# The q, k and v loads of twelve head pairs issued from ScalarE's queue instead of SyncE's, with new ranks for the order of all instructions

## The chip, the cores and the metric

The kernel runs on one core of a Trainium2 chip. The metric is device time in microseconds (us) from the start to the end of one execution. A core has five engines that work side by side, each through its own list of instructions in order: TensorE (PE in the profile, with its weight loads shown apart as PEld), VectorE (DVE), ScalarE (ACT), GpSimd (POOL) and SyncE (SP). SyncE computes nothing; its list consists of transfers (DMA) that it issues, and the profile shows it as SPq. A transfer issued by ScalarE stands in ScalarE's own list, among its computations (ACTq). All transfers run on the core's 16 DMA engines.

## What is computed

Attention over 4 batches of 8 heads, with q averaged over pairs of rows, and a gated two-layer network on its output:

```python
B, H, S, D = 4, 8, 1152, 64
q_pool = q.reshape(B, H, S // 2, 2, D).mean(axis=3)
scores = np.matmul(q_pool, k.transpose(0, 1, 3, 2)) / np.sqrt(D)
attn = softmax(scores)                    # over the last axis, 1e-9 added to the sum
x = np.matmul(attn, v).transpose(0, 2, 1, 3).reshape(2304, 512)
h = x @ w_in                              # w_in: 512 x 2048
out = (h * sigmoid(1.702 * h)) @ w_out    # w_out: 2048 x 512
```

Inputs and output are float32.

## The kernel before

The 32 heads are taken as 16 pairs (P = 0 to 15, four to a batch), and each pair is cut into nine score tiles of up to 128 rows by 1152 keys: n = 9P to 9P + 8, 144 in all. Pairs 0 to 3 ("wide") work in float32 and transpose on TensorE. Pairs 4 to 15, the **twelve later pairs**, split each operand into two float16 parts and transpose by DMA.

For a later pair the work is this. `q_load`, `k_load` and `v_load` bring q (three DMAs), k and v (one each) from memory into `qraw` (one buffer), `kraw` (one buffer) and `vraw` (two buffers). `q_add` (GpSimd, L448) adds the row pairs of q. Maxima and scales follow on VectorE, then the splits `q_hi`, `k_hi`, `v_hi` and `q_lo`, `k_lo`, `v_lo`. `q_tr` and `k_tr` are DMA transposes issued by SyncE (L547, L543), into `qT` and `kT`. A new `q_load` may start only when the former pair's `q_tr` has read `qraw`, and a `k_load` when the former `k_lo` has read `kraw`.

For each score tile n there follow: S (scores, TensorE, L693 for the later pairs), M (scaling, copy out of PSUM and row maximum, VectorE, L707), B (a small addition, ScalarE, L740), E (exponential, ScalarE, L714), H (`p_hi`, the high float16 part into a buffer `hl`, four buffers, ScalarE, L257), L (`p_lo`, the low part into the same buffer, GpSimd or VectorE, L748), T (`p_tr`, a DMA transpose of `hl` into `pt`, issued by SyncE, L761). When four tiles are transposed, `pv` (TensorE, L774) multiplies them with v.

Between these, TensorE works on the network: `h` pieces (six matmuls, L996) and `o` pieces (three matmuls, L1032), 288 of each. They need whole batches of x, so they fill gaps of a later pair's attention, and what is left of them runs behind the last score tile. ScalarE and VectorE do the gate (`tanh` L1004, `gate` L1010, `g_hi`, `g_lo` L1021), and SyncE stores the output (L1047).

The order on every engine is fixed before the program runs. The class `Plan` holds all pieces of work with an estimated duration, what they come after, the buffers they take and a rank; `Plan.order` simulates the engines and, whenever one is free, gives it the piece of the lowest rank among those that can start soon. The table `rank` says how far a kind of work stands ahead of or behind its tile; `movable` lists the kinds that may go to another engine; `wait` and `slack` are further weights of that simulation. In the program each engine then executes its list strictly in order and waits at each piece for what it needs. So a load in SyncE's list starts only when all transposes ahead of it have been issued, and each of those waits for its L.

Of the kernel before, what the change touches and what calls it, by code (L numbers as in the profile page):

```python
# [141 lines left out]
def kernel(  # L142
# [26 lines left out]
    nc = tc.nc  # L169
# [17 lines left out]
    rank = dict(  # L187
        w1=1865.4109269161, w1_rate=669.6352215416, w2=2677.1753665833, w2_rate=0.0023087894,
        w1_cut=1631.5317541564, w1_cut_rate=613.7055382454, w2_cut=-32.5791686736, w2_cut_rate=30.5602451484,
        v_max=860.0945280997, load=-14.5343009418, prep=556.0904376951, max=-2582.9885400672,  # L190
        exp=972.7441165849, p_hi=284.2709380703, p_lo=2243.1182350523, pv=1142.4802547388, x=925.9243816604,
        recip=2446.2725570035, w_tr=228.0055134896, w_ev=1267.7732570402, g=-1700.558705141,
        pv_b=-1144.7706645013, max_b=1484.9170056827, p_lo_b=1438.9279995691, prep_b=-2262.503153536,
        v=1284.3640449616, lift=75.4772111863,
    )
    movable = dict(DVE=('w_ev', 'v_hi', 'moe_hi', 'q_hi'), POOL=('p_lo', 'denom'))
    wait = dict(PE=0.071466, ACT=0.063566, DVE=0.051711, POOL=1.725535)
    slack = dict(PE=0.100951, ACT=1.016305, DVE=1.084473, POOL=1.138194, SP=1.01349, stay=1.645697, land=1.035543)
    sizes = dict(
# [142 lines left out]
    for i in range(32):  # L342
        c, kk = divmod(i, 4)
        j = c // 4
        first, last = i % 16 == 0, i % 16 == 15
# [59 lines left out]
    def heads(x, g):  # L405
        return x[g.b, 2 * g.pr:2 * g.pr + 2]

    def k_head(queue, g, a):
        queue.dma_start(out=T["kraw", g.P][:, a], in_=heads(k, g)[a].rearrange("(p r) d -> p r d", r=KR))

    def k_load(g):
        t = new("kraw", ("kraw", g.P), [128, 2, KR, D], F32)
        if g.P:
            nc.sync.dma_start(
                out=t.rearrange("p a r d -> p a (r d)"), in_=heads(k, g).rearrange("a (p r) d -> p a (r d)", r=KR)
            )
            return
        k_head(nc.scalar, g, 0)

    def q_load(g):  # L420
        t = new("qraw", ("qraw", g.P), [128, NJ, 2, D], F32)
        full, last = heads(q, g)[:, 0:1024], heads(q, g)[:, 1024:S]
        if g.P:
            nc.sync.dma_start(
                out=t[:, 0:8].rearrange("p (a j) r d -> p a (j r d)", a=2),
                in_=full.rearrange("a (p x) d -> p a (x d)", x=8),
            )
        else:
            for a, queue in enumerate((nc.sync, nc.scalar)):
                queue.dma_start(  # L430
                    out=t[:, 4 * a:4 * a + 4].rearrange("p j r d -> p (j r d)"),
                    in_=full[a].rearrange("(p x) d -> p (x d)", x=8),
                )
        for a in range(2):
            nc.sync.dma_start(
                out=t[64 * a:64 * (a + 1), NJ - 1].rearrange("p r d -> p (r d)"),
                in_=last[a].rearrange("(i r) d -> i (r d)", r=2),
            )
# [127 lines left out]
    def v_load(g):  # L566
        t = new("vraw", ("vraw", g.P), [128, 2, KR, D], F32)
        nc.sync.dma_start(
            out=t.rearrange("p a r d -> p a (r d)"), in_=heads(v, g).rearrange("a (p r) d -> p a (r d)", r=KR)
        )  # L570
# [26 lines left out]
    for g in pairs:  # L597
        n0, G = g.n0, g.P
# [6 lines left out]
        for i, what in enumerate("qkv"):  # L605
            key = (what + "raw", G)
            at, after = n0 + rank["load"] + 0.1 * i, [("E", n0 - 14 + i)] if n0 > 14 else []
            if what == "v" and g.wide:
                at, after = n0 + rank["v"] - 4, [("E", n0 - 5)] if n0 >= 5 else [("k_load", 0)]
            fn = dict(q=q_load, k=k_load, v=v_load)[what]  # L610
            plan.add(
                (what + "_load", G), "ACT" if what == "k" and not G else "SP", (2.9 if what == "q" else 1.6) if G > 3 else 1.6 if what == "q" else 0.8, at,
                lambda g=g, fn=fn: fn(g), after, take=[(what + "raw", key)], dma=2.0,
# [563 lines left out]
```

## Time and profile before

| | us |
|---|---|
| median of three runs (796.25 to 797.83) | 797.82 |
| the profiled execution: its own time | 796.32 |
| its span in the trace | 794.5 |
| TensorE busy | 757.8 (95%) |
| VectorE busy | 581.8 (73%) |
| ScalarE busy | 593.7 (75%) |
| GpSimd busy | 269.8 (34%) |

The profiled execution took 1.8 us more than its span, for what lies around the traced instructions, and 1.5 us less than the median of the runs. "Busy" of TensorE covers the whole of each matmul in the pipeline, so it is no measure of how near the engine is to its peak. Transfers are not busy time of the engine that issues them: the span of a DMA instruction on SPq or ACTq is the time that the queue was occupied with issuing it, and "landing" is when its data has arrived. The clock of TensorE was at its higher level, 2.4 GHz, almost throughout (0.995 in the mean).

In time the execution has three parts: pairs 0 to 3 with the preparation of the weights up to about 165 us, the later pairs from there to the last scores at 658 us, and the rest of the network to the end.

### The profile page before, as it was taken

What the parts mean: (1) busy time and instruction counts of PE and PEld (TensorE: products, weight loads), DVE (VectorE), ACT (ScalarE), POOL (GpSimd) and SP (SyncE); (2) the same over time, 40 slices, a digit from 0 to 9 for tenths busy, and PEclk for the clock granted to TensorE, in tenths of its full rate; (3) what the DMA queues carried; (4) which work ended last, traced back from release to release, by engine and by line L of the source; (5) the groups of instructions that cost most, each with busy time, mean ns of one, the idle gap of its engine ahead of it and who ended that gap; (6) DMA issues with size and microseconds to landing.
All of it is one profiled execution on the core that took longest, in us unless ns stands there. A gap on an engine that the chain in (4) does not pass through costs nothing.

```text
span 794.5 us, 16688 instructions
## 1 busy us (share of the span) xinstructions
PE 757.8 (95%) x6716; PEld 510.4 (64%) x6716; DVE 581.8 (73%) x915; ACT 593.7 (75%) x1005; POOL 269.8 (34%) x172
## 2 busy tenths in 40 slices
PE   6999999899999999889999998899999999999998
PEld 4556555457676767566666675567676766766664
DVE  5977898988978978668878787898889675222222
ACT  5987998989897979787888878776889786232222
POOL 2231323145566553455433233323535243000000
PEclk9999999999999999999999999999999999999999
DMA  8543343738999999999999999999999979010000
GB/s 307 194 135 114 137 140 133 193 88 178 224 185 198 208 208 204 215 203 215 184 214 198 206 197 196 222 190 227 199 221 192 176 120 176 1 28 2 28 1 26
DMA packets 331309, 128.75 MB, mean 162 GB/s; under 512 B 310496, under 2 KB 312544, under 8 KB 331232
## 3 DMA queue, kind: packets, MB, share of 16 engines
q1 hardware_dynamic: 330944, 127.13, 78.7%
q8 instruction: 52, 0.85, 0.4%
q10 hardware_dynamic: 288, 0.56, 0.2%
q14 instruction: 25, 0.20, 0.1%
HBM read 45.09 MB, written 4.72 MB: 63 GB/s over the span
## 4 chain that ended last, share of the span: by engine, by line
PE 63%; DMA 11%; ACT 9%; DVE 7%; issue 5%; SPq 2%; POOL 2%; DVEq 0%; ACTq 0%; POOLq 0%
PE h L996 16%; PE o L1032 15%; PE s L693 7%; DMA pt<-hl 7%; PE pv L774 6%; PE pv L809 5%; PE s L664 4%; PE o L786 4%; DVE p L707 2%; ACT p L714 2%; ACT hl L257 2%; PE h L313 2%; POOL hl L748 2%; PE tr L821 1%; DMA qraw<-in_q_dram 1%
## 5 line engine op out<-in xcount | busy, mean ns | idle before, releaser
L748 POOL TENSOR_TENSOR hl<-p,hl 128x1152 f16<-128x1152 f32 x72 | 177.4, 2467 | 180.1 <-ACT hl L257 160.2
L707 DVE TENSOR_SCALAR_CACHE_REDUCE p<-s,e_s 128x1152 f32<-128x1152 f32 x144 | 203.2, 1411 | 29.6 <-PE s L693 16.0
L1032 PE MATMUL o<-wbuf,g 128*128 128x512 f16 x864 | 205.0, 379 | 0.0
L996 PEld LDWEIGHTS <-wbuf 128*128 128x128 f16 x1728 | 168.9, 98 | 40.3 <-issue 4.9
L714 ACT ACTIVATE p<-p,nm 128x1152 f32<-128x1152 f32 x144 | 180.1, 1251 | 4.9 <-DVE p L707 1.2
L257 ACT ACTIVATE hl<-p 128x1152 f16<-128x1152 f32 x108 | 124.6, 1155 | 24.4 <-DMA pt<-hl 23.7
L1032 PEld LDWEIGHTS <-g 128*128 128x128 f16 x864 | 83.3, 98 | 84.9 <-issue 1.4
L693 PE MATMUL s<-kT,qT 128*128 128x384 f16 (+1 forms) x720 | 123.5, 327 | 10.2 <-DVE p L707 10.1
L996 PE MATMUL h<-x16a,wbuf 128*128 128x256 f16 x960 | 115.7, 273 | 1.6 <-DVE gf L1010 1.2
L1010 DVE SCALAR_TENSOR_TENSOR gf<-th,h 128x512 f32<-128x512 f32 x72 | 49.2, 684 | 91.2 <-ACT th L1004 91.1
L1004 ACT ACTIVATE th<-h,t_s 128x512 f32<-128x512 f32 x72 | 49.0, 681 | 83.0 <-PE h L996 82.7
L693 PEld LDWEIGHTS <-qT 128*128 128x128 f16 (+1 forms) x720 | 62.9, 100 | 55.4 <-issue 19.7
L996 PE MATMUL h<-wbuf 128*128 128x256 f16 x768 | 92.3, 275 | 1.1 <-DVE gf L1010 1.1
L774 PEld LDWEIGHTS <-vhl 128*64 128x64 f16 x1944 | 82.7, 111 | 8.8 <-DMA pt<-hl 7.6
L774 PE MATMUL pv<-pt,vhl 128*64 128x256 f16 x1296 | 76.7, 273 | 6.4 <-DMA pt<-hl 6.3
L1021 DVE SCALAR_TENSOR_TENSOR g<-gf,g 128x512 f16<-128x512 f32 x72 | 58.3, 810 | 19.0 <-ACT g L257 18.6
L308 POOL TENSOR_TENSOR wbuf<-raw 128x512 f32<-128x512 f32 x32 | 33.6, 1058 | 80.6 <-ACT raw L304 80.5
L748 DVE TENSOR_TENSOR hl<-p,hl 128x1152 f16<-128x1152 f32 x36 | 51.4, 1427 | 9.0 <-ACT hl L257 8.7
L786 PE MATMUL o<-idf,p 128*128 128x128 f32 x324 | 51.7, 288 | 5.3 <-ACT pt L257 3.0
L257 ACT ACTIVATE g<-gf 128x512 f16<-128x512 f32 x64 | 39.8, 621 | 19.2 <-DVE gf L1010 19.1
L448 POOL TENSOR_TENSOR qs<-qraw 128x576 f32<-128x576 f32 (+1 forms) x18 | 25.8, 1441 | 83.0 <-DMA qraw<-in_q_dram 64.6
L786 PEld LDWEIGHTS o<-idf,p 128*128 128x128 f32 x324 | 35.9, 143 | 24.8 <-ACT pt L257 10.1
(98 smaller groups left out, 817.8 us busy)
## 6 DMA issues: line engine op xcount, KB each, us to landing
vraw<-in_v_dram SPq DMA_DIRECT2D x16, 576.0 KB, 6.5
kraw<-in_k_dram SPq DMA_DIRECT2D x15, 576.0 KB, 5.7
raw<-in_moe_w_in_dram SPq DMA_DIRECT2D x16, 512.0 KB, 5.2
raw<-in_moe_w_out_dram SPq DMA_DIRECT2D x16, 512.0 KB, 5.3
qraw<-in_q_dram SPq DMA_DIRECT2D x15, 512.0 KB, 4.3
out_dram<-osb SPq DMA_DIRECT2D x16, 256.0 KB, 3.0
pt<-hl SPq DMA_TRANSPOSE x96, 5.0
qraw<-in_q_dram SPq DMA_DIRECT2D x32, 32.0 KB, 4.0
```

The lines of the kernel that those rows point to most:

```text
L257: nc.scalar.activation(out=out, in_=in_, func=ACTF.Copy, scale=1.0 if scale is None else scale)
L693: nc.tensor.matmul(out=ps[m, c, 0:384], lhsT=st, rhs=T["kT", g.P][:, o:o + 3].rearrange("p r c -> p (r c)"), start=(l == 0), stop=(l == 1),)
L707: nc.vector.tensor_scalar(out=p, in0=s, scalar1=e_s[:, g.P:g.P + 1], scalar2=None, op0=ALU.mult, op1=ALU.min, accum_out=m)
L714: nc.scalar.activation(out=p, in_=p, func=ACTF.Exp, bias=T["nm", n], scale=-1.0, accum_out=sm)
L748: (nc.vector if e == "DVE" else nc.gpsimd).tensor_tensor(out=t[:, 1, :], in0=T["p", n].rearrange("p c f -> p (c f)"), in1=t[:, 0, :], op=A ...
L774: nc.tensor.matmul(out=ps[64 * a:64 * (a + 1), 0:w], lhsT=T["vhl", g.P][:, a, g.block[a][c], m], rhs=pt[:, l * KR + c, o:o + w], start=(pa ...
L786: nc.tensor.transpose(ps[:, 128 * i:128 * (i + 1)], T["p", n][:, c, 128 * i:128 * (i + 1)], idf)
L996: nc.tensor.matmul(out=h[:, e, :], lhsT=w1(2 * j + e, l, kk), rhs=x_rhs(blk, m, kk), start=(kk == 0 and l == 0 and m == 0), stop=(kk == KD ...
L1004: nc.scalar.activation(out=t, in_=T["h", blk, j].rearrange("p e n -> p (e n)"), func=ACTF.Tanh, scale=t_s[:, b:b + 1])
L1010: nc.vector.scalar_tensor_tensor(out=gf, in0=T["th", blk, j], scalar=1.0, in1=T["h", blk, j].rearrange("p e n -> p (e n)"), op0=ALU.add, o ...
L1021: nc.vector.scalar_tensor_tensor(out=g[:, 1].rearrange("p e n -> p (e n)"), in0=T["gf", blk, j], scalar=2.0 ** -16, in1=g[:, 0].rearrange( ...
L1032: nc.tensor.matmul(out=o, lhsT=g[:, l, e, 128 * t:128 * (t + 1)], rhs=w2(fc, m), start=(fc == 0 and l == 0 and m == 0), stop=(fc == KFF - ...
```

## The change

`load_on` names the engine that issues a load: ScalarE for q, k and v of the pairs that aren't wide (and, as before, for half of the first pair's k), SyncE otherwise. `queue` gives the engine's handle, and `k_load`, `q_load` and `v_load` use it. In the plan a load on ScalarE counts 1.6 us for q and 0.55 us for k or v. The numbers of `rank`, `wait` and `slack` are other ones throughout (one line of the table is shown), and six more kinds of work may go to VectorE.

```diff
-        exp=972.7441165849, p_hi=284.2709380703, p_lo=2243.1182350523, pv=1142.4802547388, x=925.9243816604,
+        exp=878.4283184652, p_hi=216.9275015825, p_lo=2273.577182275, pv=1249.4892793623, x=851.3221790499,
...
-    movable = dict(DVE=('w_ev', 'v_hi', 'moe_hi', 'q_hi'), POOL=('p_lo', 'denom'))
+    movable = dict(DVE=('w_ev', 'moe_hi', 'x_hi', 'w_hi', 'p_hi', 'qk_ev', 'k_hi', 'w_sign', 'q_hi'), POOL=('p_lo', 'denom'))
...
+    def load_on(what, g):
+        return "ACT" if what in "qkv" and not g.wide or what == "k" and not g.P else "SP"
+
+    def queue(what, g):
+        return nc.scalar if load_on(what, g) == "ACT" else nc.sync
...
     def k_load(g):
-            nc.sync.dma_start(
+            queue("k", g).dma_start(
...
     def q_load(g):
-            nc.sync.dma_start(
+            queue("q", g).dma_start(
...
         for a in range(2):
-            nc.sync.dma_start(
+            queue("q", g).dma_start(
...
     def v_load(g):
-        nc.sync.dma_start(
+        queue("v", g).dma_start(
...
             plan.add(
-                (what + "_load", G), "ACT" if what == "k" and not G else "SP", (2.9 if what == "q" else 1.6) if G > 3 else 1.6 if what == "q" else 0.8, at,
+                (what + "_load", G), load_on(what, g),
+                (1.6 if what == "q" else 0.55) * (1.8 if G > 3 and load_on(what, g) == "SP" else 1.0), at,
```

The program that comes out has the same pieces of work in another order. Of the 144 tiles' and 16 pairs' pieces these change engine: 60 load DMAs go from SyncE to ScalarE; ScalarE has 16 H fewer (92 for 108), which VectorE does; ten L go from VectorE to GpSimd (82 for 72); all twelve `v_hi` are on ScalarE (six before); four `k_hi`, five `x_hi` and a few others go to VectorE.

On SyncE, from pair 7's `q_tr` to the loads of pair 8, before (qT, kT are the pair's transposes, pt those of the score tiles):

```order
L547 DMA_TRANSPOSE qT_3128<-qraw_2789 128x18x128
L543 DMA_TRANSPOSE kT_3212<-kn_3101 128x18x128
L761 DMA_TRANSPOSE pt_3079<-hl_3011 128x18x128
L761 DMA_TRANSPOSE pt_3283<-hl_3139 128x18x128
L761 DMA_TRANSPOSE pt_3283<-hl_3246 128x18x128
L424 DMA qraw_3352<-in_q_dram 128x2x512
L435 DMA qraw_3352<-in_q_dram 64x128 x2
L761 DMA_TRANSPOSE pt_3387<-hl_3276 128x18x128
L414 DMA kraw_3442<-in_k_dram 128x2x576
L568 DMA vraw_3476<-in_v_dram 128x2x576
L761 DMA_TRANSPOSE pt_3387<-hl_3320 128x18x128
```

and now, from the same pair's `q_tr` on:

```order
L553 DMA_TRANSPOSE qT_3159<-qraw_2762 128x18x128
L768 DMA_TRANSPOSE pt_3101<-hl_3103 128x18x128
L549 DMA_TRANSPOSE kT_3238<-kn_3056 128x18x128
L768 DMA_TRANSPOSE pt_3319<-hl_3164 128x18x128
L768 DMA_TRANSPOSE pt_3319<-hl_3198 128x18x128
L768 DMA_TRANSPOSE pt_3402<-hl_3317 128x18x128
L768 DMA_TRANSPOSE pt_3402<-hl_3385 128x18x128
L768 DMA_TRANSPOSE pt_3530<-hl_3434 128x18x128
```

The five DMAs of pair 8 are gone from the list, and transposes of score tiles follow one another there.

On ScalarE, at the place of pair 8's loads, before (p are exponentials, hl the H, nm the B, th and g belong to the network):

```order
L714 ACTIVATE p_3148,w_d_86<-p_3148,nm_3147 128x1152
L1004 ACTIVATE th_3271<-h_3232,t_s_84 128x512
L257 ACTIVATE hl_3276<-p_3148 128x1152
L257 ACTIVATE g_3292<-gf_3278 128x512
L740 ACTIVATE nm_3264<-nm_3264,add_c_90 128x1
L726 ACTIVATE w_r_87<-w_d_86,add_c_90 128x4
L714 ACTIVATE p_3265,w_d_86<-p_3265,nm_3264 128x1152
```

and now:

```order
L721 ACTIVATE p_3201,w_d_86<-p_3201,nm_3200 128x1152
L430 DMA qraw_3262<-in_q_dram 128x2x512
L441 DMA qraw_3262<-in_q_dram 64x128 x2
L1011 ACTIVATE th_3315<-h_3204,t_s_84 128x512
L257 ACTIVATE wbuf_70<-wbuf_70,x_r_83 128x2x512
L257 ACTIVATE xt_3335<-tr_3240 128x64
L257 ACTIVATE g_3337<-gf_3325 128x512
L747 ACTIVATE nm_3302<-nm_3302,add_c_90 128x1
L257 ACTIVATE vhl_3347<-vraw_2214,s_qkv_73 128x18x64
L721 ACTIVATE p_3303,w_d_86<-p_3303,nm_3302 128x1152
L747 ACTIVATE nm_3343<-nm_3343,add_c_90 128x1
L420 DMA kraw_3377<-in_k_dram 128x2x576
```

The loads stand between ScalarE's computations, k two exponentials behind q; v follows four instructions after k. With q stand behind it the `tanh` of a network piece and the B and E of the next tile.

Against the score tiles the loads stand earlier: `q_load` of pairs 8 to 15 follows the scores of the tile 13 before the pair's first (10 to 12 before it until now), its `q_add` two tiles later (11 or 12 ahead of the pair; until now 9 to 11, one tile after the load), and `q_tr` 7 to 8 tiles ahead of it (5 to 7 until now). T mostly follows its tile's scores by two or three tiles (three or four until now).

On TensorE the pieces of the network lie elsewhere: 41 of the 576 `h` and `o` pieces stand ahead of pair 5's first scores (26 until now), 333 between those and the last scores (359), and 202 behind the last scores (191).

## Rows read from the trace of the kernel before

**Rows 1.** Busy time by engine from 200 to 600 us, then PEclk, DMA share, GB/s.

```profile
200.00:600.00 400.00, 380.16 (x3712) 264.61 (x3712) 334.04 (x489) 329.26 (x538) 173.66 (x94) 1.00 1.11 205
```

**Rows 2.** TensorE's waits, 150 to 650 us: total us, times, longest.

```profile
PE s L693 <- DVE p L707: 10.1, 13, 1.6
PE pv L774 <- DMA pt<-hl: 6.3, 5, 3.4
```

**Rows 3.** The chain of waits, 275 to 345 us: start, duration, what.

```profile
275.32 3.10 POOL hl L748
278.42 1.83 SPq L761
...
284.34 3.86 DMA qraw<-in_q_dram
...
288.37 1.41 POOL qs L448
...
289.87 8.70 DMA pt<-hl
...
329.42 10.25 DMA pt<-hl
```

**Rows 4.** Timeline of SyncE's queue, one pair's loads: start, duration, what.

```profile
326.44 0.53 SPq L424 DMA_DIRECT2D qraw<-in_q_dram  x1
327.04 1.14 SPq L435 DMA_DIRECT2D qraw<-in_q_dram  x2
328.22 0.59 SPq L414 DMA_DIRECT2D kraw<-in_k_dram  x1
328.91 0.41 SPq L568 DMA_DIRECT2D vraw<-in_v_dram  x1
```

**Rows 5.** Line 761's transposes, 200 to 600 us: ns shortest/median/longest; landing likewise.

```profile
L761 SPq DMA_TRANSPOSE pt<-hl x75: 2467/2952/7819, 206.4 to 592.5; - x75
...
DMA to landing us min/median/max: 4.5/5.2/11.0
```

**Rows 6.** Tile qraw, 200 to 600 us: its loads, and who waited for it.

```profile
L424 SPq DMA_DIRECT2D qraw<-in_q_dram x10: 432/534/538, 204.7 to 571.6; - x10
...
POOL qs L448: 43.8, 10
```

**Rows 7.** Timeline of TensorE after two pairs' loads; in brackets the idle time before.

```profile
336.10 1.14 PE L693 MATMUL s<-kT,qT 128*128 128x384 f16 x6 [0.91 <-DVE p L707]
...
508.42 1.14 PE L693 MATMUL s<-kT,qT 128*128 128x384 f16 x6 [1.10 <-DVE p L707]
```

**Rows 8.** Groups by line and form: busy us, mean ns of one, idle before.

```profile
L748 DVE TENSOR_TENSOR hl<-p,hl 128x1152 f16<-128x1152 f32 x36 | 51.4, 1427 | 9.0 <-ACT hl L257 8.7
...
L257 ACT ACTIVATE hl<-p 128x1152 f16<-128x1152 f32 x108 | 124.6, 1155 | 24.4 <-DMA pt<-hl 23.7
...
L261 DVE TENSOR_SCALAR vhl<-vraw,s_qkv 128x1152 f16<-128x1152 f32 x6 | 8.4, 1392 | 0.0
```

**Rows 9.** Timeline of ScalarE's, then SyncE's transfers at the start.

```profile
0.73 0.41 ACTq L409 DMA_DIRECT2D kraw<-in_k_dram  x1
1.17 0.46 ACTq L430 DMA_DIRECT2D qraw<-in_q_dram  x1
...
0.73 0.39 SPq L430 DMA_DIRECT2D qraw<-in_q_dram  x1
```

**Rows 10.** Busy time by stretch, columns as in Rows 1: transposes alone, then mixed.

```profile
606.00:628.00 22.00, 22.00 (x201) 15.43 (x199) 15.91 (x19) 18.13 (x32) 10.27 (x5) 1.00 1.19 193
...
371.60:378.00 6.40, 6.40 (x62) 4.53 (x57) 4.93 (x8) 4.53 (x8) 4.72 (x4) 1.00 1.08 245
```

**Rows 11.** TensorE: the last scores, and four network pieces behind them.

```profile
657.71 1.14 PE L693 MATMUL s<-kT,qT 128*128 128x384 f16 x6
...
688.91 2.62 PE h L996 x24
```

**Rows 12.** Group of the `o` matmuls, 658 to 795 us; last is idle before.

```profile
L1032 PE MATMUL o<-wbuf,g 128*128 128x512 f16 x297 | 68.1, 379 | 0.0
```

More of the change, by code (lines that the diff above doesn't have):

```diff
@@ L187 @@
     rank = dict(
-        w1=1865.4109269161, w1_rate=669.6352215416, w2=2677.1753665833, w2_rate=0.0023087894,
-        w1_cut=1631.5317541564, w1_cut_rate=613.7055382454, w2_cut=-32.5791686736, w2_cut_rate=30.5602451484,
-        v_max=860.0945280997, load=-14.5343009418, prep=556.0904376951, max=-2582.9885400672,
-        exp=972.7441165849, p_hi=284.2709380703, p_lo=2243.1182350523, pv=1142.4802547388, x=925.9243816604,
-        recip=2446.2725570035, w_tr=228.0055134896, w_ev=1267.7732570402, g=-1700.558705141,
-        pv_b=-1144.7706645013, max_b=1484.9170056827, p_lo_b=1438.9279995691, prep_b=-2262.503153536,
-        v=1284.3640449616, lift=75.4772111863,
-    )
-    movable = dict(DVE=('w_ev', 'v_hi', 'moe_hi', 'q_hi'), POOL=('p_lo', 'denom'))
-    wait = dict(PE=0.071466, ACT=0.063566, DVE=0.051711, POOL=1.725535)
-    slack = dict(PE=0.100951, ACT=1.016305, DVE=1.084473, POOL=1.138194, SP=1.01349, stay=1.645697, land=1.035543)
+        w1=1992.4881419666, w1_rate=0.3088697376, w2=2782.8562607731, w2_rate=0.1021909337,
+        w1_cut=1673.0709993249, w1_cut_rate=0.0034826828, w2_cut=-201.3257245865, w2_cut_rate=20.5323112849,
+        v_max=722.3898967545, load=-377.6522261757, prep=732.6815723084, max=-2831.4193236673,
+        exp=878.4283184652, p_hi=216.9275015825, p_lo=2273.577182275, pv=1249.4892793623, x=851.3221790499,
+        recip=2600.7039151482, w_tr=640.673544478, w_ev=1281.6711227968, g=-1825.404513894,
+        pv_b=-1250.0594996229, max_b=1346.1944998637, p_lo_b=1605.391158808, prep_b=-1839.7624530306,
+        v=1544.1640303766, lift=-0.6394915734,
+    )
+    movable = dict(DVE=('w_ev', 'moe_hi', 'x_hi', 'w_hi', 'p_hi', 'qk_ev', 'k_hi', 'w_sign', 'q_hi'), POOL=('p_lo', 'denom'))
+    wait = dict(PE=0.175109, ACT=0.096407, DVE=0.036059, POOL=0.015854)
+    slack = dict(PE=0.335663, ACT=1.014485, DVE=1.057966, POOL=1.146382, SP=1.018385, stay=15.331489, land=1.230748)
     sizes = dict(
@@ L428, in q_load @@
         else:
-            for a, queue in enumerate((nc.sync, nc.scalar)):
-                queue.dma_start(
+            for a, first in enumerate((nc.sync, nc.scalar)):
+                first.dma_start(
                     out=t[:, 4 * a:4 * a + 4].rearrange("p j r d -> p (j r d)"),
```

## The prediction

> **What bounds the kernel now.** I began with busy time by stretch. In the later pairs, 200 to 600 us, TensorE is busy for 380 of 400 us, VectorE for 334, ScalarE for 329, and the DMA share is 1.11 [rows 1]. So TensorE is idle for 20 us there; that is nearly all that this stage can give back. In the last part nothing is to be had: the network's matmuls follow one another with no idle time before them [rows 12].
>
> Next, what the 20 us wait for. The list of waits names two sources: scores that wait for VectorE to copy the former ones out (10.1 us, 13 times), and `pv` that waits for a transposed tile (6.3 us, 5 times) [rows 2].
>
> Then the chain of waits, to see what is behind these. From 275 to 345 us it hardly touches TensorE. It goes from an L on GpSimd into SyncE's queue, there to q's load, from its landing to `q_add` on GpSimd, and on to transposes that took 8.70 and 10.25 us to land [rows 3], where the median is 5.2 [rows 5]. This is a ring through lists that run in order: the load stands behind transposes that wait for GpSimd's L, and `q_add` stands in GpSimd's list ahead of the next L and waits for the load. GpSimd sat 43.8 us at `q_add` in ten pairs [rows 6].
>
> **What the change removes.** Per pair, SyncE loses one q load of 0.53 us, two of together 1.14, k with 0.59 and v with 0.41: 2.67 us [rows 4], in twelve pairs 32 us, of which only what reaches TensorE counts.
>
> First term: `pv`'s 6.3 us. The longest of its five waits is 3.4 us [rows 2], so the other four share 2.9. All four fall away if a transpose is issued 2.67 us earlier, and 0.7 of the long one stays. I take 5.6 us as gained.
>
> Second term: the gaps just after a pair's loads. I count six, three after the loads at 326 us and three after those at 495 us, from 0.91 us before the scores at 336.10 to 1.10 before those at 508.42 [rows 7], together 5.3 us. Their cause is the ring: L is late because `q_add` holds GpSimd, and the next transposes land late. In the new order `q_add` stands two tiles behind its load instead of one, and one tile is about 4.5 us: the ten loads lie (571.6 - 204.7) / 9 = 40.8 us apart [rows 6], for nine tiles. That covers the 4.4 us that GpSimd waited in the mean. But the bytes still pass through the same DMA engines, so late landings remain; I take half, 2.7 us. Bounds of both terms: 0, if the transfers take as long whatever queue they come from, and 11.6.
>
> **What it adds.** ScalarE gets 60 issues. Its own two at the start took 0.41 and 0.46 us [rows 9], and SyncE's took up to 0.59 [rows 4], so 26 to 35 us, say 28. It gives up 16 H of 1.155 us [rows 8], 18.5 us; the other moves nearly cancel. So about 10 us more on an engine busy for 82% of the stage, behind which the next B and E queue, and behind those L, T and `pv`. VectorE does the 16 H; the same form on it took 1.392 us in the mean (22.3 us), and it gives up ten L of 1.427 us (14.3) [rows 8]: 8 us more. An issue or an H costs TensorE time only where an E or an M was next in line for the scores. Between none of these 18 us and the size of the wait for VectorE today, 10.1 us [rows 2], doubled, I take 2 us: a fifth more of that wait, somewhat over the few per cent that the engines' load grows by.
>
> A load now waits in ScalarE's list for its buffer. Between `q_tr` and the next `q_load` stand three transposes and some 15 of ScalarE's instructions; I cost it at nothing, since a transpose lands in 5.2 us and 15 instructions there with two or three exponentials and conversions take more. If SyncE lags by more than those, everything behind the load on ScalarE stops with it, `tanh` and the next E first.
>
> **What it moves.** Eleven more network pieces stand behind the last scores (202 for 191). Four pieces of `h` took 2.62 us [rows 11], so one takes 0.655 and eleven 7.2. They aren't new work, only later. So the last scores, now at 657.7 us [rows 11], must begin at 650.5 for no change at all. Between pair 5's first scores and the last ones stand 26 fewer pieces, 17.0 us in eleven pairs: each pair must get 1.5 us shorter than 40.8, or TensorE idles more than today. The first part (pairs 0 to 3) has the same exponentials and evictions in another order; I take it as equal, with 3 us to either side.
>
> **The sum** against the profiled execution of 796.3 us: -5.6 - 2.7 + 2.0 = -6.3, so 790.0. The median of the runs is 1.5 us above that execution: **791.5 us**, 0.8% faster.
>
> **A rule against it.** Until here the relief is one of SyncE's list. The DMA engines ran at a share of 1.11 with 205 GB/s in the whole stage [rows 1], transposes alone reached 193 GB/s and loads mixed with transposes 245 [rows 10]. The Trainium skill, "DMA: Bandwidth & Descriptors", section "Issuing engines are not separate DMA queues", says that transfers begun by several engines run on the same 16 DMA engines and that only the issuing sequencer's time is saved. By that page the second term would be 0 and the result 794.2. The rows bear it out in part: the share leaves little room, but 245 is well above 205.
>
> **The rivals.**
>
> *No room in the DMA engines (slower).* If they carry no more than the 205 GB/s of today, the pairs cannot be shorter than 40.8 us: all relief of the queue turns into waits for landings, the last scores stay at 657.7, and the eleven pieces come on top: 797.8 + 7.2 = 805.0. For it: the share of 1.11 through the stage. Against it: 245 GB/s in a mixed stretch. It decides at 40.8 - 1.5 = 39.3 us per pair, that is 205 x 40.8 / 39.3 = 213 GB/s; at 216 my forecast holds. Chance 0.20.
>
> *ScalarE's loads wait for SyncE's transposes (slower).* Two DMAs issued at 0.73 us by both engines took 0.41 and 0.39 us, no longer than alone [rows 9]; but neither was a transpose, and of a load on ScalarE beside a transpose the trace has no row. A transpose occupies SyncE for 2.95 us in the median [rows 5], eleven to a pair, 32 of 40.8 us. If a load had to wait for the running one, it would meet one 8 times in 10 and wait half of it: 1.2 us, five times a pair, 6 us on ScalarE. With its 329 / 400 of 40.8 us, 33.6, and 0.8 for the moves above, that makes 40.4 us. An engine that waits for others as ScalarE does will not run without gaps; at nine tenths busy a pair takes 44.9. Against the 39.3 needed that is 1.1 to 5.6 us per pair, in eleven pairs 12 to 62 us: 810 to 860, most likely the lower half. It decides where ScalarE's extra wait exceeds about 1 us a pair. Chance 0.16. The Trainium skill has this as a rule: "Perfetto Trace Analysis", section "DMA Instruction — HWDGE (DVE, Sync)", says that the block which makes descriptors is shared by the issuing sequencers, locked for one instruction at a time, and that the recorded span includes the wait for the lock. The start of the trace shows no such wait, and no row shows a transpose beside another engine's DMA.
>
> *Even.* Only `pv`'s first term comes in, and ScalarE and VectorE take most of it back: 796.2 to 799.4. Chance 0.12.
>
> *The loads don't move.* The order shows all 60 in ScalarE's list, so this falls out.
>
> **How the numbers follow.** Forecast 0.52, with 783 to 796: the low end is all 11.6 us of the two terms and 3 us from the first part. A measurement of this kernel can tell some 0.2%, 1.6 us, from no change. Faster is the forecast alone, 0.52; same 0.12; slower both rivals, 0.36. The range reaches from 783 to 808: it leaves out the end below the forecast (0.03) and nearly all of the second rival (0.15).
>
> **What would show each step.** SyncE's queue: no gap between transposes at the loads, and the longest transpose issue, now 7.8 us [rows 5], shorter. GpSimd's 43.8 us at `q_add` mostly gone. `pv`'s wait for `pt` near 1 us. ScalarE's load issues at 0.4 to 0.6 us each; at 1.5 us or more the second rival is right. GB/s of the stage at 213 or above; at 205, with longer landings, the first rival is right. The last scores at about 644 us. I am wrong if they begin after 650.5, or if the first part takes some 3 us longer than now.

## The result, and the profile after

The changed kernel took 806.7 us in the median of 14 runs (794.2 to 814.0), the kernel before beside it 796.3 us (794.1 to 800.4, 14 runs). The ratio is 1.0056, with a 95% interval of 1.0028 to 1.0083: slower by about 0.6%, where 0.8% faster was forecast. The changed kernel scatters three times as widely as the one before; ratios here leave out, of each kernel, the runs more than 1.5% above its fastest, so that a median can lie further from 796 than its ratio says.

The profiled execution of the changed kernel took 805.2 us, span 803.4, against 796.3 and 794.5: 8.9 us more. Three lines of TensorE's timeline divide them: the first scores of tile 36, the last scores, and what is left behind them. First the changed kernel's (start, duration, what):

```profile
168.72 1.14 PE L700 MATMUL s<-kT,qT 128*128 128x384 f16 x6
...
659.40 1.14 PE L700 MATMUL s<-kT,qT 128*128 128x384 f16 x6
```

In the kernel before, the scores of tile 36 began at 165.23 and the last ones at 657.71 [rows 11]. So the first part is 3.5 us longer, the later pairs take 490.7 us instead of 492.5, 1.8 shorter, and what follows takes 144.0 instead of 136.8, 7.2 longer. The last is eleven pieces of 0.655 us, as the prediction had it; the network still runs there without a gap (group of the `o` matmuls from 660 us on in the changed kernel; the last number is the idle time before):

```profile
L1039 PE MATMUL o<-wbuf,g 128*128 128x512 f16 x312 | 71.5, 379 | 0.0
```

Where the later pairs lose time is read from busy time by stretch (columns as in [rows 1]). The kernel before:

```profile
0.00:200.00 200.00, 187.28 (x1386) 115.45 (x1387) 164.43 (x303) 174.07 (x320) 62.72 (x62) 0.99 0.55 162
200.00:400.00 200.00, 191.45 (x1878) 133.21 (x1877) 166.85 (x242) 169.18 (x276) 103.75 (x54) 0.99 1.11 204
400.00:600.00 200.00, 188.71 (x1836) 131.40 (x1835) 167.19 (x248) 160.08 (x263) 69.91 (x41) 1.00 1.11 206
```

The changed kernel, and as its last row the stretch of [rows 1]:

```profile
0.00:200.00 200.00, 186.90 (x1355) 115.83 (x1356) 170.45 (x313) 169.39 (x307) 64.39 (x61) 0.99 0.52 156
200.00:400.00 200.00, 178.30 (x1708) 124.12 (x1707) 162.19 (x238) 146.54 (x244) 98.66 (x52) 0.96 1.08 201
400.00:600.00 200.00, 194.66 (x1990) 137.84 (x1990) 165.54 (x259) 164.19 (x272) 107.32 (x55) 1.00 1.13 215
...
200.00:600.00 400.00, 372.96 (x3696) 261.96 (x3697) 327.73 (x496) 310.74 (x515) 205.98 (x106) 0.98 1.11 208
```

TensorE idles 21.7 us between 200 and 400 us, against 8.6 before, and gets 6 of these 13 us back after 400 us (5.3 against 11.3). The granted clock is 0.96 in the worse stretch. The DMA share stays at 1.11, and the rate rises from 205 to 208 GB/s, where the prediction needed 213.

TensorE's waits from 150 to 650 us in the changed kernel (total us, times, longest) answer [rows 2]:

```profile
PE pv L781 <- DMA pt<-hl: 17.3, 6, 6.2
PE s L700 <- DVE p L714: 9.0, 8, 1.6
```

The wait of `pv` for a transposed tile, 6.3 us before, has become 17.3. Three of its six waits in TensorE's timeline (in brackets the idle time before):

```profile
259.92 4.80 PE L781 MATMUL pv<-pt,vhl 128*64 128x256 f16 x53 [3.31 <-DMA pt<-hl]
...
337.41 4.91 PE L781 MATMUL pv<-pt,vhl 128*64 128x256 f16 x44 [4.77 <-DMA pt<-hl]
...
383.37 4.91 PE L781 MATMUL pv<-pt,vhl 128*64 128x256 f16 x53 [6.20 <-DMA pt<-hl]
```

The transposes behind it (in the changed kernel line 768; ns shortest, median, longest) answer [rows 5]: the longest issue is shorter than 7819, but the landing is later, 6.1 us in the median for 5.2:

```profile
L768 SPq DMA_TRANSPOSE pt<-hl x76: 2263/3315/6602, 199.2 to 591.1; - x76
...
DMA to landing us min/median/max: 4.5/6.1/13.1
```

The loads, now on ScalarE, in the lines of the two parts of q's load (form as above), answer [rows 4, 6]:

```profile
L441 ACTq DMA_DIRECT2D qraw<-in_q_dram x20: 568/768/1608, 212.5 to 570.8; - x20
...
L430 ACTq DMA_DIRECT2D qraw<-in_q_dram x10: 369/374/438, 212.1 to 569.8; - x10
```

GpSimd's wait for q's load, 43.8 us in ten pairs before [rows 6], in the changed kernel's list of waits from 200 to 600 us:

```profile
POOL qs L454 <- DMA qraw<-in_q_dram: 28.8, 8, 8.4
```

### The profile page after: what moved, and what is told of

It reads as the page before. It is cut to its first block, busy times and chain, and to the rows that moved or that the text cites. A ratio compares the mean times of both kernels' runs of the same rounds, so it can differ in the third digit from the quotient of the medians.

```text
span 803.4 us, 16712 instructions
## 1 busy us (share of the span) xinstructions
PE 759.3 (95%) x6716; PEld 513.9 (64%) x6716; DVE 583.8 (73%) x935; ACT 576.5 (72%) x975; POOL 299.3 (37%) x182
## 5 line engine op out<-in xcount | busy, mean ns | idle before, releaser
L755 POOL TENSOR_TENSOR hl<-p,hl 128x1152 f16<-128x1152 f32 x82 | 209.3, 2554 | 192.4 <-ACT hl L257 112.2
L257 ACT ACTIVATE hl<-p 128x1152 f16<-128x1152 f32 x92 | 106.4, 1156 | 19.4 <-DMA pt<-hl 18.4
L781 PEld LDWEIGHTS <-vhl 128*64 128x64 f16 x1944 | 86.8, 115 | 21.2 <-DMA pt<-hl 19.3
L781 PE MATMUL pv<-pt,vhl 128*64 128x256 f16 x1296 | 83.0, 286 | 17.3 <-DMA pt<-hl 17.3
L1028 DVE SCALAR_TENSOR_TENSOR g<-gf,g 128x512 f16<-128x512 f32 x72 | 62.0, 862 | 18.1 <-ACT g L257 17.9
L747 ACT ACTIVATE nm<-nm,add_c 128x1 f32<-128x1 f32 x108 | 31.0, 287 | 36.8 <-DVE p L714 28.3
L257 ACT ACTIVATE g<-gf 128x512 f16<-128x512 f32 x61 | 38.0, 623 | 21.5 <-DVE gf L1017 21.5
L671 PE MATMUL s<-kT,qT 64*128 64x512 f32 (+3 forms) x240 | 50.3, 531 | 0.9 <-DVE p L714 0.9
```

Of the source, the lines that this page charges most:

```text
L257: nc.scalar.activation(out=out, in_=in_, func=ACTF.Copy, scale=1.0 if scale is None else scale)
L671: nc.tensor.matmul(out=ps[m, bank, 0:128 * (last - first)], lhsT=qT[h, (j - half) % NJ, m], rhs=kT[h, first:last].rearrange("p j c -> p (j ...
L755: (nc.vector if e == "DVE" else nc.gpsimd).tensor_tensor(out=t[:, 1, :], in0=T["p", n].rearrange("p c f -> p (c f)"), in1=t[:, 0, :], op=A ...
L781: nc.tensor.matmul(out=ps[64 * a:64 * (a + 1), 0:w], lhsT=T["vhl", g.P][:, a, g.block[a][c], m], rhs=pt[:, l * KR + c, o:o + w], start=(pa ...
L1028: nc.vector.scalar_tensor_tensor(out=g[:, 1].rearrange("p e n -> p (e n)"), in0=T["gf", blk, j], scalar=2.0 ** -16, in1=g[:, 0].rearrange( ...
```

## Experiments

The change has two halves, the queue and the order that the planner makes from the new table and costs. The first experiments take them apart; the next ones ask what sets the length of the later pairs' stage, from the first scores of tile 36 to the last scores; the others move parts of the order. One table holds the profiled runs: the stage, TensorE's busy and other time in it, the rate of its transfers, the pieces of the network planned behind the last scores, and the span; then the median of all runs and the ratio to the kernel before on the same chip.

| kernel | stage us | busy | not busy | GB/s | pieces behind | span us | median us (runs) | ratio, 95% |
|---|---|---|---|---|---|---|---|---|
| before | 492.5 | 471.9 | 20.6 | 194 | 191 | 794.5 | 796.3 (14) | |
| changed | 490.7 | 462.6 | 28.1 | 196 | 202 | 803.4 | 806.7 (14) | 1.0056 (1.0028 to 1.0083) |
| e1, old order, new queue | 490.6 | 472.3 | 18.3 | 195 | 191 | 792.7 | 795.0 (12) | 0.998 (0.9953 to 1.0007) |
| e2, new order, old queue | 498.7 | 467.9 | 30.9 | 193 | 202 | 810.3 | 811.2 (4) | 1.0169 (1.0147 to 1.0191) |
| e3, H on ScalarE | 489.0 | 461.9 | 27.2 | 197 | 202 | 801.3 | 806.6 (4) | 1.0116 (1.0088 to 1.0144) |
| e4, `pv` later | 512.1 | 467.7 | 44.4 | 186 | 204 | 824.9 | 826.1 (4) | 1.0368 (1.0337 to 1.0398) |
| e5, e1 and 6.3 MB more | 522.5 | 481.1 | 41.4 | 194 | 191 | 824.3 | 822.7 (2) | 1.0328 (1.0284 to 1.0372) |
| e6, old table planned anew | 505.8 | 475.9 | 29.9 | 192 | 192 | 806.0 | 807.8 (6) | 1.014 (1.0111 to 1.0169) |
| e7, SyncE's cost up | 524.1 | 477.8 | 46.3 | 183 | 192 | 829.1 | 830.8 (6) | 1.0434 (1.0402 to 1.0466) |
| e8, e1 and 5.9 MB fewer | 480.0 | 468.4 | 11.7 | 187 | 191 | 782.6 | 785.3 (2) | 0.9859 (0.9829 to 0.9889) |
| e9, e1, 11 pieces later | 513.5 | 475.0 | 38.5 | 187 | 202 | 823.5 | 821.6 (6) | 1.0304 (1.0267 to 1.0341) |
| e10, e1, 20 pieces later | 524.7 | 474.5 | 50.3 | 183 | 211 | 840.1 | 834.7 (4) | 1.0469 (1.0441 to 1.0497) |
| e11b, paced as before | 550.5 | 485.3 | 65.2 | 175 | 191 | 854.8 | 851.7 (6) | 1.066 (1.0612 to 1.0707) |
| e12, changed and 5.9 MB fewer | 481.9 | 461.5 | 20.4 | 188 | 202 | 793.7 | 796.0 (10) | 0.9979 (0.9954 to 1.0004) |
| e13, first piece at tile 40 | 506.0 | 472.6 | 33.4 | 190 | 201 | 816.4 | 816.7 (4) | 1.021 (1.013 to 1.029) |
| e14, first piece at tile 42 | 506.8 | 467.6 | 39.2 | 189 | 207 | 821.6 | 825.3 (4) | 1.0359 (1.0292 to 1.0427) |
| e15, e1, 10.4 us less work | 496.9 | 464.8 | 32.0 | 193 | 191 | 799.2 | 802.7 (4) | |
| e16, changed, 10.4 us less work | 499.7 | 460.9 | 38.8 | 193 | 202 | 812.2 | 808.0 (4) | 1.01 (1.0051 to 1.015) |

### Queue or order: e1 and e2

e1 is the kernel before, with only the twelve later pairs' loads on ScalarE, in the four places where they are issued:

```
-            nc.sync.dma_start(
+            (nc.sync if g.wide else nc.scalar).dma_start(
```

> The order of before, piece by piece; only the 60 load DMAs of the twelve later pairs are issued by ScalarE, at the same place in the program. Theory A (the queue: loads on a ring of their own share the DMA engines with the transposes, which then land later): slower than before by 0.5 to 1.5%, 800 to 808 us, median issue of a transpose 3.2 us or more in 200 to 600 us (2.95 before), pv waits for pt 12 us or more (6.3 before). Theory B (the order): as before or faster, 788 to 797 us, pv waits for pt 6 us or less. My prediction's own terms say 790.

e2 is the changed kernel with the loads back on SyncE, in the same order:

```
     def queue(what, g):
-        return nc.scalar if load_on(what, g) == "ACT" else nc.sync
+        return nc.sync
```

> The order of the changed kernel, piece by piece; only the 60 load DMAs are issued by SyncE, at the same place in the program. Theory A (the queue): 792 to 799 us, as before or faster, median issue of a transpose near 2.95 us, pv waits for pt below 8 us. Theory B (the order): slower than before like the changed kernel or more, 800 to 812 us, pv waits for pt 15 us or more.

The queue gains in both orders: 1.8 us of the span in the old one (794.5 to 792.7; the ratio's interval includes 1) and 6.9 in the new one (810.3 to 803.4). The order loses: 1.7% with the old queue, and with the new one 803.4 against 792.7 (ratios of 1.0056 and 0.998). So the change is slower by its order and not by its queue.

The spans of e2 divide the order's loss against the kernel before: 2.3 us in the first part, 6.2 in the stage, although 8.5 us of TensorE's work have left it, and 7.2 behind the last scores. The queue then takes 8.0 us off that stage and adds 1.2 to the first part. But the waits of e2, 150 to 650 us, are others than expected, 2.5 us for `pt` where 15 or more were named:

```profile
PE s L700 <- DVE p L714: 16.3, 9, 5.4
PE tr L481 <- DVE qkv L469: 10.7, 6, 3.7
PE pv L781 <- DMA pt<-hl: 2.5, 4, 0.9
```

So the wait of `pv` for `pt`, 17.3 us in the changed kernel, belongs to the new order together with the new queue; with the old queue the same order loses its time at the scores' copy-out and at the maxima of k and v on VectorE.

e1 also shows the first term of the sum by itself. What waited for tile `pt` in e1 from 200 to 600 us, and its transposes (forms of [rows 5]):

```profile
L761 SPq DMA_TRANSPOSE pt<-hl x75: 2402/3122/8762, 203.7 to 591.0; - x75
...
ACT hl L257: 10.1, 6
...
PEld L774: 0.7, 2
```

`pv` has no wait for `pt` left but 0.7 us at a weight load, as forecast. But TensorE's time not busy in the stage fell by 2.3 us only, from 20.6 to 18.3. Others took the place in e1's list of waits, 150 to 650 us, and the copy-out of the scores kept 8.6 of its 10.1:

```profile
PE s L693 <- DVE p L707: 8.6, 11, 1.8
PE tr L475 <- DVE qkv L463: 3.6, 1, 3.6
PE h L996 <- POOL wbuf L865: 3.1, 1, 3.1
```

GpSimd's wait for q's load did not fall either, in e1 from 200 to 600 us 50.2 us for 43.8 [rows 6]: the queue alone does not undo the ring of the second term.

```profile
POOL qs L448 <- DMA qraw<-in_q_dram: 50.2, 10, 8.1
```

### VectorE's H, and `pv`'s place: e3 and e4

e3 gives the 16 H that the new order moved to VectorE back to ScalarE, at the same places:

```
-            t["fn"](e) if t["free"] else t["fn"]()
+            t["fn"]("ACT" if t["name"][0] == "H" else e) if t["free"] else t["fn"]()
```

> The changed kernel with its 16 H that stand on VectorE done by ScalarE at the same place in the program. If those H hold up VectorE's copies of the scores or the L behind them (theory C): 3 us or more faster than the changed kernel, below 802 us. Theories A and B: no change beyond the changed kernel's own scatter, 800 to 810 us.

e4 tells the planner that `pv` may only stand behind the scores of five tiles later, so that the transposes have more time; with this condition the whole order is planned anew:

```
-    ... ready + pv_last + [("w_recip", g.P, u)],
+    ... ready + pv_last + [("w_recip", g.P, u)] + ([] if g.whole else [("S", min(n + (5, 5, 5)[u], NT - 1))]),
```

> The changed kernel's ranks, with one condition more in the plan: a pv of a later pair comes only after the scores of the tile five behind its last one. The plan then puts 11.8 pieces of TensorE's work in the mean between the last transpose that a pv needs and the pv, for 9.9 in the changed kernel and 9.0 before. If pv's place in the order is what makes it wait (theory B): pv waits for pt below 8 us for 17.3, 793 to 799 us. Theory A: the waits move to other places, 800 to 810 us.

In e3 `pv` waits 18.2 us for `pt` in 150 to 650 us, and the time is that of the changed kernel: H on VectorE is not the cause. In e4 this wait falls to 6.4 us (second row of e4's waits in the same stretch), but the wait for the scores' copy-out rises to 25.8 (first row), and the stage takes 21 us more:

```profile
PE s L700 <- DVE p L714: 25.8, 20, 4.8
PE pv L781 <- DMA pt<-hl: 6.4, 3, 3.1
```

So this attempt did not take the 17.3 us off by themselves; since the order changed throughout, it does not show that nothing could.

### What sets the stage: e5, e8, e12, e15, e16

e5 is e1 with two loads more for each later pair, 24 of 262 KB, into a tile that nobody reads; e8 is e1 without the ten loads of v of pairs 6 to 15, and e12 the changed kernel without them:

```
e5  +  if u < 2 and not g.wide:
    +      nc.scalar.dma_start(out=more, in_=heads(v, g).rearrange("a (p r) d -> p a (r d)", r=KR)[:, :, 0:4 * D])
e8, e12
    +  if g.P >= 6:
    +      T["vraw", g.P] = T["vraw", g.P - 2]
    +      return
```

> The order of before with the loads on ScalarE (795.0 us), and 24 more loads of 262 KB, two to a later pair, from ScalarE's queue into a tile that nothing reads: 6.3 MB more through the DMA engines. If the DMA engines have no room (first rival), 6.3 MB at 205 GB/s make the later pairs 31 us longer: last scores near 686 us, 820 to 828 us. If they have room, only the issues and some late landings cost: last scores before 662 us, 795 to 802 us.

> The order of before with the loads on ScalarE (795.0 us), without the v loads of pairs 6 to 15: each uses the v of the pair two before, so ten loads of 590 KB, 5.9 MB, are left out and the output is another one; all other work is the same. If the DMA engines bound the later pairs (first rival): at 205 GB/s up to 29 us less, down to where TensorE's own work (472 us of the 491) binds: last scores at 640 to 648 us, 777 to 787 us. If they don't: last scores after 652 us, 790 us or more.

> The changed kernel without the loads of v for pairs 6 to 15 (5.9 MB fewer; those pairs compute with an earlier pair's v, so the output is not the reference's; every other instruction stays). Theory of the full DMA engines: in the old order the same bytes were worth 10.1 us of the span (792.7 to 782.6); here, where TensorE idles 13 us more between 200 and 400 us, at least as much: 789 to 796, with the wait of pv for the transposed weights under 8 us in 150 to 650 (17.3 with the loads). Rival (the waits are set by the order of the instructions, whatever the bytes): the wait of pv stays above 13 us and the time above 800.

Busy time of the stage by engine, columns as in [rows 1]. First e5:

```profile
164.89:687.43 522.54, 481.11 (x4674) 331.10 (x4672) 405.93 (x605) 411.43 (x675) 216.59 (x118) 0.97 1.05 194
```

Then e1, with 194 to 195 GB/s like it:

```profile
165.24:655.83 490.59, 472.26 (x4672) 328.18 (x4671) 403.23 (x606) 410.65 (x675) 219.34 (x117) 0.99 1.07 195
```

And e8:

```profile
165.84:645.87 480.03, 468.38 (x4672) 327.03 (x4672) 406.75 (x606) 410.60 (x675) 216.97 (x117) 1.00 1.02 187
```

6.3 MB more cost 31.9 us at the same rate, which is what they take at 197 GB/s: the DMA engines had no room for them. Nothing waited for these loads to land, and their issues took 0.37 us each in the median. Of the 31.9 us, 23.1 are idle time of TensorE and 8.8 the same matmuls taking longer, at a granted clock of 0.97 for 0.99. 5.9 MB fewer gave 10.6 us in the old order and, in the changed kernel (e12), 8.8 of the stage and 9.7 of the span (803.4 to 793.7), not the 30 that they take at that rate. Not all of the 30 could come back: TensorE had 18.3 us of the stage idle in e1 and 28.1 in the changed kernel, and without these loads it still has 11.7 (e8) and 20.4 (e12). In e12 `pv` still waits 10.0 us for `pt`, between the two theories' bounds: bytes are part of that wait, not all of it.

e15 and e16 take 10.4 us of TensorE's own work out of the stage, of e1 and of the changed kernel: 24 `o` pieces are cut from three matmuls to one.

```
-        for l, m in ((0, 0), (0, 1), (1, 0)):
+        for l, m in ((0, 0), (0, 1), (1, 0))[:1 if blk < 4 and 0 < j < 7 and i == 0 else 3]:
```

> The old order with the loads on ScalarE's queue, and 24 of the network's o pieces between tiles 41 and 108 cut from three matmuls to one (their two low-order terms are left out, so the output is less exact): 48 matmuls of 0.217 us, 10.4 us of TensorE's work, leave the stage of the later pairs; the order, the transfers and the work behind the last scores stay. Theory of the stage that TensorE doesn't set (which makes eleven pieces moved to the end cost their full 7.2 us): first to last scores stay at 488 to 493 us, the time at 793 to 797. Theory that TensorE's work sets it: 480 to 482 us, and 784 to 787; then moving pieces out of the stage should have been free.

> The changed kernel with the same 48 matmuls left out (24 o pieces cut from three matmuls to one, so the output is less exact). Stage not set by TensorE: first to last scores stay at 488 to 493 us and the profiled time near 805, within the changed kernel's own scatter. Set by TensorE: 480 us, and 10 us less.

e15's four runs lie between 787.9 and 808.2 us, with a median of 802.7; e1's twelve between 790.9 and 804.4, with 795.0. None of the four reaches the 784 to 787 of the theory that TensorE's work sets the stage, though the lowest comes within 1 us of it; between the lowest of each kernel there are 3.0 us, not 10.4. e16's four lie between 801.0 and 814.0, within the changed kernel's own 794.2 to 814.0, and are no lower in the median (808.0 for 806.7). The two profiled runs, 801.0 and 814.0 us, lie 13 us above the lowest of their kernel, so their stages of 496.9 and 499.7 us are no measure. So in these orders work taken from TensorE hardly shortens the time: with four runs each, at most a third of the 10.4 us shows in the lowest runs and nothing in the medians. That TensorE's work does not set the stage is made likely by this, not measured closely.

### Other orders: e6, e7, e9, e10, e11b, e13, e14

e6 is the changed kernel planned with the tables of the kernel before (`rank`, `movable`, `wait`, `slack`), e7 with one factor changed:

```
e7  -  slack = dict(..., SP=1.018385, ...)
    +  slack = dict(..., SP=1.15, ...)
```

> The changed kernel (loads on ScalarE, planned there) with the table of before: rank, movable, wait and slack. The plan leaves 192 pieces of the network behind the last scores (191 before, 202 in the changed kernel). If the new table is what makes the changed kernel slower: 790 to 798 us, last scores before 658 us. If any order that the plan makes for loads on ScalarE loses: 800 us or more.

> The changed kernel with one number of the plan changed: SyncE's pieces count 15% more than their estimate instead of 1.8%, so a transpose counts 3.3 us, which is the median of the changed kernel's trace, instead of 2.95. The plan then leaves 192 pieces behind the last scores instead of 202. Theory D (the plan took the pairs for shorter than they are and left work of the network for the end, while the pairs' length does not hang on that work): last scores still at 657 to 661 us and 796 to 800 us. If the ten pieces lengthen the pairs by their own time: last scores at 664 us or later, 802 to 808 us.

e6 leaves 192 pieces for the end and still takes 807.8 us: this order, planned from the old table, lost too, so the new table alone is not the cause. e7 went outside of both expectations. Its stage takes 524 us at 183 GB/s, which no theory here had foreseen.

e9 and e10 keep e1's order and let the network's stream run later from tile 85 on (`pieces` is 14 in e9 and 24 in e10), so that 11 and 20 pieces more stand behind the last scores:

```
+    def later(order, tile=85, pieces=14):
+        at = [t["name"] for t, _ in order].index(("S", tile))
+        slots = [i for i in range(at, len(order)) if order[i][0]["name"][0] in NET]
+        work, held = [order[i] for i in slots], 0
+        while pieces:
+            pieces -= order[slots[held]][0]["name"][0] in "ho"
+            held += 1
+        gone, rest = set(slots[:held]), dict(zip(slots[held:], work))
+        return [rest.get(i, x) for i, x in enumerate(order) if i not in gone] + work[len(work) - held:]
```

> The order of before with the loads on ScalarE (795.0 us, 191 pieces of the network behind the last scores); from tile 85 on every piece of the network and what hangs on it stands some eleven pieces later in the program, all else unmoved: 202 pieces behind the last scores, as in the changed kernel (98 h, 104 o). Theory D (the later pairs are as long as the DMA engines need, so pieces taken out of them come on top at the end): last scores at 655 to 658 us as in the run without this, 801 to 804 us. If TensorE's work sets the pairs' length: last scores near 649 us, 795 us.

> The same with some twenty pieces: 211 behind the last scores, 20 more than the 191, 13.1 us of TensorE's work. Theory D: last scores at 655 to 658 us, 807 to 810 us. If TensorE's work sets the pairs' length: 795 us.

Both lose far more than 0.655 us a piece, and more than either theory expected. In e9 30.8 us of the span against e1: 22.9 in the stage, the rest behind it (144.8 us for 136.9). Its waits show a load that came late: TensorE's list, 150 to 650 us, and VectorE's in the same stretch.

```profile
PE s L693 <- DVE p L707: 17.8, 19, 3.5
PE tr L475 <- DVE qkv L463: 11.7, 2, 10.3
```

```profile
DVE qkv L463 <- DMA vraw<-in_v_dram: 9.5, 1, 9.5
```

e11b puts the network's pieces of the changed kernel back between the same tiles as before, by a list of counts per tile; e13 and e14 let the planner hold the first block's pieces back to tile 40 or 42:

```
e13 -  xs + wh + ([("h", blk, j, i - 1)] if i else ([("h", *prev, 3)] if seq > 2 else [])),
    +  xs + wh + ([("h", blk, j, i - 1)] if i else ([("h", *prev, 3)] if seq > 2 else [])) + ([("S", 40)] if blk == 0 else []),
```

> The changed kernel with one thing put back: from tile 36 on, the network's pieces stand between the same two tiles' scores as in the kernel before, except some ten that wait for their input at tiles 126 and 138 to 140 (none before tile 40, 26 before tile 45 where the changed kernel has 41, 191 behind the last scores where it has 202). The loads stay on ScalarE's queue, the rest of the new order stays. Theory E (the new order spends 15 pieces at tiles 36 to 44, where TensorE has no gaps; the first transposes of the later pairs start later by that, and the pieces are missing as cover between 200 and 400 us, where TensorE idles 21.7 us against 8.6): the idle time of 200 to 400 us falls below 14, and the time is 794 to 799. Theory F (the loss is in where the new order puts the attention's own steps: k and q transposes, pv, the splits; the pieces only follow): the waits of 200 to 400 us stay, and the time is 803 to 810. Theory G (an order that no planner went over loses by itself, as the shifted ones did): above 810.

> The changed kernel planned anew with one condition more: no piece of the network's first block ahead of the scores of tile 40 (15 pieces ahead of tile 44, as in the kernel before with 14; the changed kernel has 29; 201 pieces behind the last scores, 202 in the changed kernel). Theory E (the pieces spent early cost the stage): the idle time of TensorE between 200 and 400 us falls from 21.7 us to below 14, and the time is 795 to 800. Theory H (an order planned by these costs scatters by more than any such part is worth, because the planner does not see how late a transfer lands when the DMA engines are full): the idle time stays at 17 to 24 us in some other places, and the time is 803 to 830.

> The same with tile 42 in place of tile 40 (4 pieces ahead of tile 44, 207 behind the last scores). Theory E: with 25 pieces fewer early than the changed kernel, the idle time between 200 and 400 us is below 14 us; 5 pieces more at the end cost 3.3 us: 798 to 803. Theory H: 803 to 830, and not in the order of the pieces spent early.

e11b tells nothing about its theories E and F: placed by hand, each `gate` stands right behind its `tanh`, and VectorE waits for it (150 to 740 us). Its time is what theory G had named, an order that loses by itself.

```profile
DVE gf L1017 <- ACT th L1011: 49.0, 29, 4.5
```

In e13 and e14, with 15 and 4 pieces ahead of tile 44 instead of 29, TensorE idles 17.5 and 19.1 us between 200 and 400 us, and both are slower than the changed kernel. Neither the idle time below 14 us nor the time of theory E came, that the early pieces were the loss. Since both orders were planned anew throughout, this speaks against theory E without ruling it out.

## Why the prediction was wrong

**The queue's relief: right in place, small in effect.** The 6.3 us that `pv` waited for `pt` go away by the queue alone, to 0.7 (e1), which is the 5.6 of the first term. The sum let them reach the last scores; in e1 these came 1.9 us sooner (657.7 to 655.8), a gain that e1's ratio, 0.998 with an interval up to 1.0007, does not set apart from none. New waits of 3.6 and 3.1 us stand in e1's list instead.

**The ring: not shown.** The second term, 2.7 us, wanted GpSimd's 43.8 us mostly gone. They became 50.2 in e1 and 28.8 in the changed kernel, where TensorE's wait for the scores' copy-out is 9.0 us for 10.1. What had waited for SyncE's list now waits for the landing: q's loads land in 5.5 us in the median in e1 and 6.3 in the changed kernel, 4.1 before (200 to 600 us). This is what the Trainium skill, "DMA: Bandwidth & Descriptors", section "Issuing engines are not separate DMA queues", said against the change; e5's 31.9 us for 6.3 MB agree with it.

**The added work: too dear.** The 2.0 us for ScalarE and VectorE do not show: the scores wait 9.0 us for VectorE's copy-out, not 12. The 16 H on VectorE were reckoned at 1.392 us, the time of v's split by another operation (TENSOR_SCALAR); they are copies (CAST) and took 0.82 us each, 13.2 in all for the 22.3 of the working (group by line and form, changed kernel):

```profile
L259 DVE CAST hl<-p 128x1152 f16<-128x1152 f32 x16 | 13.2, 823 | 1.9 <-DMA pt<-hl 1.9
```

ScalarE's computing fell from 329 to 311 us between 200 and 600 us (issues are not counted in it), and the issues lie beside what it computes, as its timeline in the changed kernel shows for two of them:

```profile
241.40 1.26 ACT L721 ACTIVATE p<-p,nm 128x1152 f32<-128x1152 f32 x1
242.15 0.37 ACTq L430 DMA_DIRECT2D qraw<-in_q_dram  x1
242.55 0.81 ACTq L441 DMA_DIRECT2D qraw<-in_q_dram  x1
...
242.65 1.24 ACT L257 ACTIVATE vhl<-vraw,s_qkv 128x1152 f16<-128x1152 f32 x1
```

That the loads wait in ScalarE's list for their buffers was costed at nothing, and that held: the longest wait of its queue ahead of a load was 0.7 us.

**The rival of the shared block: fell.** ScalarE's load issues took 0.37 us (first part of q, median) to 1.61 (longest of the last parts), beside transposes of 2.3 to 6.6 us on SyncE. One at 242.15 us took 0.37 (above) while this transpose was recorded on SyncE's queue:

```profile
240.01 2.76 SPq L549 DMA_TRANSPOSE kT<-kn  x1
```

So a load does not wait until the recorded span of a transpose is over, and the wait of 1.2 us per load that the rival reckoned did not come. The rule named there, from "Perfetto Trace Analysis" of the Trainium skill, section "DMA Instruction — HWDGE (DVE, Sync)", speaks of a lock on the block that makes descriptors; the trace excludes one held for a transpose's whole recorded span, and not a shorter one. The last parts of q's load took 0.77 us each in the median, where two together took 1.14 on SyncE's queue [rows 4].

**The first part: at the bound.** It was taken as equal, with 3 us to either side, and became 3.5 us longer. Two network pieces that stand ahead of tile 36 now are 1.3 of it.

**The step that failed: the eleven pieces costed at nothing.** "They aren't new work, only later" holds only if the stage that they leave gets shorter by them, and the working said itself that each pair had to get 1.5 us shorter. It did not: 490.7 us with 13 pieces (8.5 us) less of TensorE's work in it, against 492.5. TensorE's time not busy there grew from 20.6 us to 28.1, where the sum took 6.3 off it. e15 and e16 point the same way: taking TensorE's work out hardly shortens the time. A stage with TensorE busy for 471.9 of 492.5 us thus did not get shorter with its work. So the eleven pieces cost their full 7.2 us, and with the first part's 3.5 and the stage's 1.8 the other way that is the 8.9 us of the profiled runs. Against the 790.0 of the sum the profiled run was 15.2 us too long: 7.2 for the pieces, 3.5 for the first part, and 4.5 because the stage gave 1.8 us and not the 6.3 of the other terms. The working had no term for waits that the new order itself brings, and e2, with the old queue, shows that there are such: its stage has 30.9 us not busy, 10.3 more than before.

That is the case of the first rival, which gave 805.0 us, by its own sign: 208 GB/s where 213 were to decide. Its reason holds in part. That the DMA engines have no room is shown by e5. That the stage is as long as its bytes is not: 5.9 MB fewer gave 10.6 and 8.8 us of it, while more idle time than that was left (e8, e12). And that its 805.0 is so near the profiled 805.2 is partly luck: it took the queue's relief as lost and the order as free, where the runs show the queue taking 8.0 us off the new order's stage and the order adding 6.2.

**What stays open.** Why the new order has 13 us more of TensorE's idle time between 200 and 400 us, at nearly the same rate (201 and 204 GB/s), is not settled. Against e1, which has the same queue, it is 10 us more (21.7 for 12.0). H on VectorE is not the cause (e3); that the pieces spent early are is not borne out (e13, e14); and holding `pv` back did not help (e4). Bytes are a part in both orders: without 5.9 MB of them the 21.7 us become 11.2 (e12) and the 12.0 become 5.9 (e8). The five other orders that the planner made with the loads on ScalarE (e4, e6, e7, e13, e14) took 808 to 831 us, and the two shifts of the old order that kept every step of the attention in place 822 and 835. TensorE's time not busy in the stage reaches from 18.3 us (e1) to 50.3 (e10) in them, so orders differ by as much as the 32 us that the change takes off SyncE's list. No version here that does the whole work was shown faster than the kernel before; e1 at 0.998, with an interval up to 1.0007, comes nearest.

## What to carry to other kernels

Work that leaves a stage makes it shorter only if that work sets its length, and a busy share of 95% doesn't show that; take a little of it out and look, over enough runs, before costing a move at nothing. When a change consists of a queue and a new order, run each alone: here the queue's gain of 2 to 7 us in the profiled runs was lost to the order that came with it. Relief of the list that issues transfers is worth what the transfers then land earlier, and beside DMA engines at a share of 1.11 that was 1.9 us of 5.6 in the profiled runs, which is within the noise.

## What the runs showed of the hardware

After a long wait TensorE paid twice here. 53 matmuls of `pv` that began after 6.20 us of idle time took 4.91 us (the line at 383.37 us above); in the kernel before, 53 of the same form after a wait of 0.49 us took 3.13 (its timeline):

```profile
387.42 3.13 PE L774 MATMUL pv<-pt,vhl 128*64 128x256 f16 x53 [0.49 <-DMA pt<-hl]
```

The granted clock (column PEclk of busy time by stretch) was 0.62 over the former, in the changed kernel, so most of that time was at 1.2 and not at 2.4 GHz:

```profile
383.40:388.20 4.80, 4.80 (x56) 4.21 (x58) 1.08 (x1) 1.35 (x2) 2.36 (x1) 0.62 0.93 193
```

and 1.00 over the latter, in the kernel before:

```profile
387.42:390.55 3.13, 3.13 (x54) 2.93 (x55) 3.13 (x7) 3.13 (x6) 1.22 (x1) 1.00 1.63 200
```

The price of bytes was not even: 31.9 us for 6.3 MB more, 10.6 for 5.9 MB fewer, from the same kernel e1. But e1 had only 18.3 us of idle time of TensorE in the stage to give back.

H, 128x1152 from float32 to float16, took VectorE 0.82 us as a CAST (changed kernel) and ScalarE 1.16 [rows 8]; v's split of the same size took VectorE 1.39 us as a TENSOR_SCALAR [rows 8].
